# Tables, weights and the first token tiles re-ordered in a spectral mixing kernel with a squared-ReLU MLP behind it

## The chip, the cores and the metric

The kernel runs on one core of a Trainium2 chip. The metric is the device time of one execution in microseconds; before the change its median over 7 runs is 849.89 us (848.02 to 851.43). The engines that compute are TensorE (PE, with its weight loads shown as PEld), VectorE (DVE), ScalarE (ACT) and GpSimd (POOL). SyncE (SP) issues transfers; POOL issues those that convert from 32-bit to 16-bit on the way.

## The reference

Eight batches of 3008 rows with 256 features. Each batch is taken to frequencies along its rows, mixed there by a complex 256 x 256 weight with a bias, shrunk towards zero by 0.01, and taken back. All rows then go through an MLP with 2048 hidden features.

```python
X = np.fft.rfft(x, axis=1)                 # x: (8, 3008, 256)
Xr, Xi = X.real, X.imag
Yr = Xr @ w_r - Xi @ w_i + b_r
Yi = Xr @ w_i + Xi @ w_r + b_i
Y = shrink(Yr, 0.01) + 1j * shrink(Yi, 0.01)   # sign(v) * max(|v| - 0.01, 0)
y = np.fft.irfft(Y, n=3008, axis=1).reshape(24064, 256)
h = y @ w_in                               # 256 x 2048
g = s * np.maximum(h, 0) ** 2 + b
out = g @ w_out                            # 2048 x 256
```

## The kernel before

**The transform.** 3008 is 94 x 32, and the DFT is done in two steps each way. The first step multiplies by a 94 x 96 table (A_t) along n1 and gives 96 rows, kept as 24 pairs; the second goes along n2 (32) with a table for each pair (F_t, and F_2, the same table with its real and imaginary halves exchanged). Mixing follows, then the inverse along n2 (T_t) and the last step along n1 (C_t). The result for one batch is yt: 2 x 128 features on partitions, 32 n2 and 94 n1 as columns. The MLP uses it as it lies.

**Batch 0** has its own routine, first_batch. x comes in four chunks (two halves each) on POOL's queue, the first step writes ut, and then 12 steps run (features in two halves ec of 128, six groups u of four pairs each): mix (W_t; the sums leave as g, half by DVE and half by ACT), fwd_dft (F_t, F_2; ACT makes m and DVE makes z, the shrunk values), inv_dft (T_t, leaves as vt). Four pairs belong to one group, so group 0 uses pairs 0 to 3. turn transposes vt by an identity matrix (eye_t) into vs, and last_dft (C_t) gives yt. Nothing of batch 0 goes through DRAM. In the second half of the steps and behind them, the first DFT step of batch 1 (s1_units, 16 units, each one matmul and one copy to a tile u) is put between; what is left of it goes into the first token tiles.

**Batches 1 to 7** go another way: s1 units store u to DRAM (ud) and load it in another order (us); s23 units do fwd, sum, mix and inverse and store v (vd), which comes back as vs in two loads; s4 units do the last step. One x chunk gives 4 of the 16 s1 units.

**The MLP** goes over token tiles of up to 512 rows. A tile has 16 slots (mc), one for each 128 hidden features. first_mm does the up-projection of a slot (two matmuls into a bank of psh); after every second slot ACT takes the ReLU of the pair (rt), and DVE (or ACT, where a running estimate of load finds it freer) squares it (gt). second_mms does the down-projection of the tile before, four matmuls a slot, into psa, and DVE adds the bias and stores (ost). The first six tiles are "wide": three take the first 16 n2 of batch 0, three the other 16.

**What sets the order.** The dictionary plan holds, for each slot, the units that are emitted ahead of its up-projection; schedule(start, span, units) spreads units evenly over span slots. Batch 1's tiles begin at slot 96 (mark[1]). The framework may then move instructions on each engine's queue within their dependences; each engine works its queue in order. PSUM has eight banks: psf (2) and psa (2), and four that are psm in first_batch and psh (2 x 2) from then on. evac gives a copy out of PSUM to ACT or DVE by the estimate of load.

**Transfers at the start.** SP: A_t, w_r, w_i (whole, 256 KB each, 32-bit staging tiles w_st), the biases, sel_t; after the first chunk of x, F_c (compact forward tables of pairs 0 to 11, L267); after the third chunk, T_t of the first half, F_t and F_2 of pairs 12 to 23, T_t of the second half, and small things (L273 to L283). One-element memsets by DVE (L392, L397) hold these transfers back until then. ACT places W (place_w, L320) and the forward tables of pairs 0 to 11 (place_f, L325; DVE does F_2, L331 and L334). POOL waits at a one-element copy (L406) for F_t of pairs 12 to 23, then issues the four x chunks of batch 1 (L213), w_in in two parts (L291) and w_out (L292). Later it makes W_g from w_st (L311 to L313) and sums w_out (L340 to L345) for the bias matmul (make_bias, L349).

The lines of the steps that matter here: s1 L570, turn L491, last_dft L511, ReLU L776, square L783, up-projection L769, down-projection L840, forward of batches 1 to 7 L606, inverse L665, store of v L674, load of vs L681, last step L718; L170 and L174 are the copies of ACT and DVE.

Of the kernel before, what the change touches and what calls it, by code (L numbers as in the profile page):

```python
# [96 lines left out]
def kernel(  # L97
# [27 lines left out]
    F_d = nc.inline_tensor(fwd[:, 0:H].astype(np.float16), name="dft_fwd").ap()  # L125
    f_all = np.zeros((P, NPAIR, 2, 2, N2))
    t_all = np.zeros((P, NPAIR, 2, 64))
    for i in range(4):
# [3 lines left out]
    f_2 = np.stack([-f_all[:, H:, 1], f_all[:, H:, 0]], axis=2)  # L132
    f_d, f_2_d, t_d = (
        nc.inline_tensor(t.reshape(P, -1, P).astype(np.float16), name=name).ap()
        for t, name in ((f_all[:, H:], "fwd_rest"), (f_2, "fwd_rest_i"), (t_all, "dft_inv"))
# [68 lines left out]
    def emit_load_x(b, first=None):  # L204
        xv = x[b].rearrange("(n1 n2) d -> n1 (n2 d)", n2=N2)
        for c in range(N2 // XCH):
            t = xpool.tile([P, XCH * D], F16, name="x16", tag="x16")
            if first is not None:
                gate = nc.gpsimd.tensor_copy(out=t[0:1, 0:1], in_=first)
            parts = 2 if b == 0 else 1  # L210
            w = XCH * D // parts
            for i in range(parts):
                nc.gpsimd.dma_start(  # L213
                    out=t[0:N1, i * w : (i + 1) * w],
                    in_=xv[:, c * XCH * D + i * w : c * XCH * D + (i + 1) * w],
                )
            x16[(b, c)] = t
# [17 lines left out]
    for w in (w_r, w_i):  # L235
        st = rpool.tile([P, DC, D], F32, name="w_st", tag="rt")
        nc.sync.dma_start(out=st, in_=w.rearrange("(c p) e -> p c e", p=P))
        w_st.append(st)

# [5 lines left out]
    F_c = uspool.tile([P, H, 2, N2], F16, name="F_c", tag="us")  # L245
# [6 lines left out]
    sel_t = cpool.tile([P, P], F16, name="sel_t")  # L252
    eye_t = cpool.tile([P, P], F16, name="eye_t")
# [12 lines left out]
    def emit_load_forward():  # L266
        nc.sync.dma_start(  # L267
            out=F_c.rearrange("p q r k -> p q (r k)"), in_=F_d
        )
        nc.sync.dma_start(out=sel_t, in_=S_d)  # L270

    def emit_load_inverse():
        nc.sync.dma_start(out=T_t[:, 0:H], in_=t_d[:, 0:H])  # L273
        nc.sync.dma_start(out=F_t[:, H:], in_=f_d)
        nc.sync.dma_start(out=F_2[1], in_=f_2_d)
        t_load = nc.sync.dma_start(out=T_t[:, H:], in_=t_d[:, H:])
        with tc.issue_after(t_load.ins):
            nc.sync.dma_start(out=eye_t, in_=E_d)
            nc.sync.dma_start(out=C_t, in_=C_d)
            for i, bv in enumerate((b_r, b_i)):  # L280
                nc.sync.dma_start(out=b_st[:, i], in_=bv.unsqueeze(0).to_broadcast([P, D]))
            nc.sync.dma_start(out=s_bc, in_=moe_s.unsqueeze(0).to_broadcast([P, 1]))
            nc.sync.dma_start(out=bb_bc, in_=moe_b.unsqueeze(0).to_broadcast([P, 1]))  # L283
# [15 lines left out]
    nc.vector.memset(F_t[:, 0:H], 0.0)  # L299
    nc.gpsimd.memset(F_2[0], 0.0)  # L300
# [14 lines left out]
    def blocks(t):  # L315
        return t.rearrange("p q (r a k) -> p q r a k", r=2, a=2)

    def place_w():
        for i in range(2):
            nc.scalar.copy(out=W_t[:, :, i], in_=w_st[i])  # L320

    def place_f():
        for a in range(2):
            r = slice(64 * a, 64 * a + 64)
            nc.scalar.copy(out=blocks(F_t)[r, 0:H, :, a], in_=F_c[r])  # L325

    def place_f_2():

        for a in range(2):
            r = slice(64 * a, 64 * a + 64)  # L330
            nc.vector.tensor_scalar_mul(  # L331
                out=blocks(F_2[0])[r, :, 0, a], in0=F_c[r, :, 1], scalar1=-1.0
            )
            nc.vector.tensor_copy(out=blocks(F_2[0])[r, :, 1, a], in_=F_c[r, :, 0])  # L334
# [28 lines left out]
    def first_batch():  # L363
# [3 lines left out]
        for g in range(N2 // 4):  # L367
# [22 lines left out]
            if c == 0:  # L390
                with tc.issue_after(last_dve.ins):
                    nc.vector.memset(F_c[0:1, 0, 0, 0:1], 0.0)  # L392
                emit_load_forward()
            if c == 2:
                with tc.issue_after(last_dve.ins):
                    for t in (T_t[:, 0:H], F_t[:, H:], F_2[1], T_t[:, H:]):
                        nc.vector.memset(t[0:1, 0, 0:1], 0.0)  # L397
                emit_load_inverse()
            if c == 1:
                with tc.issue_after(last_act.ins):  # L400
                    place_w()
        with tc.issue_after(last_dve.ins), tc.issue_after(last_act.ins):
            place_f()
            place_f_2()

        gate = nc.gpsimd.tensor_copy(out=w_in_t[0][0:1, 0:1], in_=F_t[0:1, H, 0:1])  # L406
        with tc.issue_after(gate.ins):
            emit_load_x(1)
            emit_load_weights()

# [75 lines left out]
        def turn(ec, k):  # L486
            for i in range(2):
                ps = any_bank() if ec else mix_bank()
                n = 8 * k + 4 * i
                for j in range(4):  # L490
                    nc.tensor.matmul(  # L491
                        ps[0:96, j * P : j * P + P], vt[:, ec, n + j, :], eye_t,
                        start=True, stop=True,
                    )
                h, n = divmod(n, HW)
                evac(
                    vs[(0, h)][:, n : n + 4, ec * P : (ec + 1) * P],
                    ps[0:96].rearrange("p (j e) -> p j e", e=P), 512,
                )

        yt = yts[0] = ypool.tile([P, DC, N2, 96], F16, name="yt", tag="yt")

        def last_dft(ec, n2):

            if ec or n2 >= 16:
                ps = [any_bank(), any_bank()]
            else:
                ps = [one_bank(), other_bank()]
            for j in range(8):
                h, k = divmod(n2 + j, HW)  # L510
                nc.tensor.matmul(  # L511
                    ps[j // 4][:, (j % 4) * 96 : (j % 4) * 96 + 96],
                    vs[(0, h)][:, k, ec * P : (ec + 1) * P], C_t,
                    start=True, stop=True,
                )
            for i in range(2):
                evac(
                    yt[:, ec, n2 + 4 * i : n2 + 4 * i + 4, :],
                    ps[i][:, 0:384].rearrange("p (j n) -> p j n", n=96), 384,
                )  # L520
# [9 lines left out]
        for i in range(2 * U + 2):  # L530
# [7 lines left out]
            if 0 <= k < 4:  # L538
                turn(0, k)
            for n in {1: (0,), 2: (8,), 4: (16, 24)}.get(k, ()):  # L540
                last_dft(0, n)
            if i >= 2 * U:
                some(3)
# [7 lines left out]
        for k in range(4):  # L551
            turn(1, k)
            some(1)
            if k:
                last_dft(1, 8 * (k - 1))
        last_dft(1, 24)
        return more

# [308 lines left out]
    with tc.tile_pool(name="psm", bufs=4, space=bass.MemoryType.PSUM) as pool:  # L867
        pools["m"] = pool
        more = first_batch()
# [11 lines left out]
    schedule(0, 10, more)  # L881
    plan.setdefault(15, []).append(make_bias)
    plan.setdefault(17, []).append(load_x_2)
    schedule(24, 42, s23_units(1))
    schedule(mark[1] - 14, 12, s4_units(1))
    for b in range(2, B):
        s0, s1, s2 = mark[b - 2], mark[b - 1], mark[b]
        p = s1 - s0
        schedule(s0 + 40, p - 48, s1_units(b))
# [48 lines left out]
```

## Time and profile before

| | us |
|---|---|
| median of 7 runs | 849.89 |
| the profiled execution | 848.6 |
| its span, first to last instruction | 846.7 |
| first x chunk half of batch 0 used by PE | 5.36 |
| first mixing matmul | 13.77 |
| first forward matmul of batch 0 | 16.55 |
| first s1 matmul of batch 1 | 38.83 |
| w_out used by POOL | 41.94 |
| first up-projection matmul | 48.05 |
| first forward matmul of batch 1 | 63.59 |
| first last-step matmul of batch 1 | 131.01 |

All times in the table and below are from the start of the span. A timeline line gives start, duration, engine, line of the kernel, operation, result and operands, shapes and number; in brackets the engine's idle time ahead of it and what ended that. Busy times of PE count pipelined matmuls, whose ends are modelled, so a full PE can still be one whose matmuls wait for each other. The chain of waits goes back from the last instruction through whatever released each step, by the latest semaphore event seen; a step may be named there that had long been enough.

### The profile page before, as it was taken

How to read it: one execution, taken by the hardware profiler on the slowest of the kernel's cores; microseconds unless marked ns; L12 is line 12 of the kernel's file. 1: busy time of each engine (PE TensorE's matmuls, PEld its weight loads, DVE VectorE, ACT ScalarE, POOL GpSimd, SP SyncE). 2: the span in 40 equal slices, each digit the busy share in tenths (PEclk: the TensorE clock that was granted, in tenths of full speed). 3: DMA queues.
4: the chain of work that ended last, by engine and by line, in shares of the span. 5: the costliest groups of instructions: out<-in, count | busy, mean ns of one | idle time of the engine just before them, and what ended most of it. 6: DMA issues, size and time to landing. Idle time of an engine off the chain costs nothing.

```text
span 846.7 us, 17115 instructions
## 1 busy us (share of the span) xinstructions
PE 834.2 (99%) x6653; PEld 599.7 (71%) x6653; DVE 692.4 (82%) x1026; ACT 642.4 (76%) x864; POOL 45.9 (5%) x71
## 2 busy tenths in 40 slices
PE   8999999999999999999999999999999999999997
PEld 6857767777677766777677776777667777766765
DVE  5989987888878987888888888798977888776674
ACT  5988887787778787788777787778877778666663
POOL 4340000000000001000000000000000000000000
PEclk9999999999999999999999999999999999999999
DMA  8955467224762367324761247613354223411111
GB/s 199 181 144 123 117 144 202 87 71 103 174 185 56 98 164 185 99 74 108 180 178 51 80 102 196 173 41 91 103 154 123 60 78 97 112 33 38 38 44 50
DMA packets 105746, 96.06 MB, mean 113 GB/s; under 512 B 9542, under 2 KB 97482, under 8 KB 104322
## 3 DMA queue, kind: packets, MB, share of 16 engines
q1 hardware_dynamic: 99218, 80.55, 33.1%
q0 software_dynamic: 6448, 14.42, 10.7%
q8 instruction: 52, 0.85, 0.4%
q14 instruction: 28, 0.23, 0.1%
HBM read 53.52 MB, written 46.66 MB: 118 GB/s over the span
## 4 chain that ended last, share of the span: by engine, by line
PE 85%; DMA 5%; DVE 4%; ACT 2%; POOL 1%; issue 1%; DVEq 0%; ACTq 0%; SPq 0%; POOLq 0%
PE psa L840 36%; PE psh L769 35%; PE psf L635 4%; DMA w_out_t<-in_moe_w_out_dram 2%; DVE gt L783 2%; PE psf L570 2%; PE psf L621 2%; PE psf L606 2%; PE psf L718 2%; PE psf L665 2%; ACT rt L776 1%; DMA vd<-v 1%; DMA vs<-vd 1%; DMA x<-in_x_dram 1%; POOL acc L344 1%
## 5 line engine op out<-in xcount | busy, mean ns | idle before, releaser
L776 ACT ACTIVATE rt<-psh 128x1024 f32<-128x1024 f32 (+2 forms) x384 | 386.6, 1008 | 120.3 <-PE psh L769 118.5
L783 DVE TENSOR_TENSOR gt<-rt 128x1024 f16<-128x1024 f32 (+2 forms) x321 | 384.7, 1202 | 98.1 <-ACT rt L776 97.4
L840 PE MATMUL psa<-w_out_t,gt 128*128 128x256 f16 (+1 forms) x3024 | 454.6, 272 | 0.5 <-DVE gt L783 0.4
L840 PEld LDWEIGHTS <-gt 128*128 128x128 f16 (+1 forms) x3024 | 300.9, 101 | 187.8 <-issue 1.7
L769 PE MATMUL psh<-yt,w_in 128*128 128x512 f16 (+1 forms) x1344 | 396.3, 378 | 0.2 <-ACT rt L776 0.2
L769 PEld LDWEIGHTS <-w_in 128*128 128x128 f16 x1536 | 142.9, 98 | 27.9 <-issue 2.4
L850 DVE SCALAR_TENSOR_TENSOR ost<-psa,s_bc,bias_bc 128x512 f32<-128x512 f32 (+2 forms) x97 | 71.1, 733 | 8.3 <-PE psa L840 7.1
L780 ACT ACTIVATE gt<-rt 128x1024 f16<-128x1024 f32 (+2 forms) x63 | 66.2, 1051 | 1.0
L640 DVE TENSOR_TENSOR ring<-psf,s 128x512 f16<-128x512 f32 x84 | 57.6, 686 | 3.7 <-PE psf L635 3.1
L170 ACT CAST v<-psf 128x512 f16<-128x512 f32 x78 | 45.3, 582 | 18.8 <-PE psf L665 18.8
L170 ACT CAST xf<-psf 128x512 f16<-128x512 f32 x82 | 47.9, 585 | 10.9 <-PE psf L606 10.9
L769 PE MATMUL psh<-tail,w_in 128*128 128x512 f16 (+1 forms) x192 | 52.1, 353 | 0.0
L170 ACT CAST u<-psf 96x512 f16<-96x512 f32 x75 | 43.4, 580 | 11.0 <-PE psf L570 10.7
L635 PE MATMUL psf<-W_g,xf 128*128 128x256 f16 x336 | 50.4, 273 | 0.0
L170 ACT CAST yt<-psf 128x480 f16<-128x480 f32 (+2 forms) x73 | 37.3, 523 | 13.7 <-PE psf L718 13.6
L213 POOL DMA_DIRECT2D x<-in_x_dram x36 | 18.7, 526 | 433.3 <-PE psf L570 431.8
L570 PE MATMUL psf<-x,A_t 94*96 94x512 f16 x103 | 39.3, 381 | 1.7 <-ACT yt L170 0.5
L646 DVE TENSOR_TENSOR ring<-ring,high 128x512 f16<-128x512 f16 x84 | 35.6, 424 | 2.3
L647 DVE TENSOR_TENSOR ring<-ring 128x512 f16<-128x512 f16 x84 | 35.6, 423 | 1.9
L645 DVE TENSOR_TENSOR ring<-ring,low 128x512 f16<-128x512 f16 x84 | 35.5, 422 | 1.6
L635 PEld LDWEIGHTS <-xf 128*128 128x128 f16 x336 | 32.9, 98 | 3.8
L718 PE MATMUL psf<-C_t,vs 96*128 96x96 f16 x448 | 33.0, 205 | 0.4 <-DMA vs<-vd 0.2
(97 smaller groups left out, 501.3 us busy)
## 6 DMA issues: line engine op xcount, KB each, us to landing
out_dram<-ost SPq DMA_DIRECT2D x152, 128.0 KB
ud<-u SPq DMA_DIRECT2D x28, 384.0 KB
us<-ud SPq DMA_DIRECT2D x28, 384.0 KB
vd<-v SPq DMA_DIRECT2D x42, 256.0 KB
vs<-vd SPq DMA_DIRECT2D x14, 768.0 KB
x<-in_x_dram POOLq DMA_DIRECT2D x28, 376.0 KB, 6.8
ring<-ring SPq DMA_DIRECT2D x280, 32.0 KB
out_dram<-ost SPq DMA_DIRECT2D x16, 120.0 KB
```

What stands on the lines that cost most here:

```text
L170: return None, nc.scalar.copy(out=dst, in_=src)
L570: nc.tensor.matmul(ps[0:96, :], A_t[0:N1, :], x16[(b, c)][0:N1, j * D : (j + 2) * D], start=True, stop=True,)
L635: nc.tensor.matmul(ps[:, r, :], xt[:, 2 - r, dc], W_g[:, dc, r], start=(dc == 0), stop=(dc == DC - 1),)
L640: nc.vector.tensor_tensor(out=t, in0=ps, in1=hold[i // 2][:, i % 2].unsqueeze(1).to_broadcast([P, 2, D]), op=ALU.add,)
L646: nc.vector.tensor_tensor(out=m, in0=m, in1=high, op=ALU.min)
L718: nc.tensor.matmul(ps[:, j * 96 : (j + 1) * 96], vs[(b, h)][:, k, ec * P : (ec + 1) * P], C_t, start=True, stop=True,)
L769: nc.tensor.matmul(o, w_in_t[dc][:, mc * P : (mc + 1) * P], r, start=(dc == 0), stop=(dc == DC - 1),)
L776: nc.scalar.activation(out=rt[:, :, 0:w], in_=ps[:, :, 0:w], func=AF.Relu)
L780: nc.scalar.activation(out=gt[:, :, 0:w], in_=rt[:, :, 0:w], func=AF.Square)
L783: nc.vector.tensor_tensor(out=gt[:, :, 0:w], in0=rt[:, :, 0:w], in1=rt[:, :, 0:w], op=ALU.mult)
L840: nc.tensor.matmul(ps[0:size, h, :], gts[(ti, mc // 2)][:, mc % 2, sub * size : (sub + 1) * size], w_out_t[:, mc, :], start=(mc == 0), sto ...
L850: nc.vector.scalar_tensor_tensor(out=ost[0:size, 0:k], in0=ps[0:size, 0:k], scalar=s_bc[0:size], in1=bias_bc[0:size, 0:k], op0=ALU.mult, o ...
```

## The change

Four things.

1. The compact forward table F_c holds 4 pairs instead of 12 and is loaded at the very start; the full tables F_t and F_2 are loaded for pairs 4 to 11 too, at the head of the tables that follow the third x chunk. W is loaded and placed by halves of e (128 output features): the first half at the start, the second behind F_t, F_2 and T_t of the first half, its two placing copies (place_w(1)) emitted at step 3. place_f and the first half of W are placed after the second x chunk.
2. POOL issues chunk 0 of batch 1's x, then w_in and w_out, then chunks 1 to 3. Its gate (still F_t of pairs 12 to 23) stands behind more transfers in SP's queue.
3. turn and last_dft work on 4 n2 at a time instead of 8. Only the first 16 n2 of the second feature half are done in first_batch; the other 16 (4 turns and 4 last steps, the list rest) go to slots 20 to 36. Of the s1 units of batch 1, 4 are emitted in first_batch instead of 10 (6 in the last two steps and 4 between the turns); the other 12, instead of 6, go to slots 8 to 20 instead of 0 to 10.
4. make_bias goes to slot 21, the x load of batch 2 to slot 21, s23 of batch 1 to slots 30 to 72 (was 24 to 66), s4 of batch 1 to 83 to 99 (was 82 to 94), s1 of batch 2 to 50 to 88 (was 40 to 88).

```diff
-    F_d = nc.inline_tensor(fwd[:, 0:H].astype(np.float16), name="dft_fwd").ap()
+    F_d = nc.inline_tensor(fwd[:, 0:4].astype(np.float16), name="dft_fwd").ap()
...
-        nc.sync.dma_start(out=st, in_=w.rearrange("(c p) e -> p c e", p=P))
+        nc.sync.dma_start(
+            out=st[:, :, 0:P], in_=w.rearrange("(c p) e -> p c e", p=P)[:, :, 0:P]
+        )
         w_st.append(st)
+    F_c = uspool.tile([P, 4, 2, N2], F16, name="F_c", tag="us")
+    nc.sync.dma_start(out=F_c.rearrange("p q r k -> p q (r k)"), in_=F_d)
...
-    def emit_load_inverse():
+    def emit_load_tables():
+        nc.sync.dma_start(out=F_t[:, 4:H], in_=f_d[:, 0 : H - 4])
+        nc.sync.dma_start(out=F_2[0][:, 4:H], in_=f_2_d[:, 0 : H - 4])
         nc.sync.dma_start(out=T_t[:, 0:H], in_=t_d[:, 0:H])
-        nc.sync.dma_start(out=F_t[:, H:], in_=f_d)
-        nc.sync.dma_start(out=F_2[1], in_=f_2_d)
+        for st, w in zip(w_st, (w_r, w_i)):
+            nc.sync.dma_start(
+                out=st[:, :, P:], in_=w.rearrange("(c p) e -> p c e", p=P)[:, :, P:]
+            )
+        nc.sync.dma_start(out=F_t[:, H:], in_=f_d[:, H - 4 :])
+        nc.sync.dma_start(out=F_2[1], in_=f_2_d[:, H - 4 :])
         t_load = nc.sync.dma_start(out=T_t[:, H:], in_=t_d[:, H:])
...
-    def place_w():
+    def place_w(ec):
+        e = slice(ec * P, ec * P + P)
         for i in range(2):
-            nc.scalar.copy(out=W_t[:, :, i], in_=w_st[i])
+            nc.scalar.copy(out=W_t[:, :, i, e], in_=w_st[i][:, :, e])
...
             if c == 1:
-                with tc.issue_after(last_act.ins):
-                    place_w()
-        with tc.issue_after(last_dve.ins), tc.issue_after(last_act.ins):
-            place_f()
-            place_f_2()
+                with tc.issue_after(last_act.ins), tc.issue_after(last_dve.ins):
+                    place_f()
+                    place_w(0)
...
         with tc.issue_after(gate.ins):
-            emit_load_x(1)
+            emit_load_x(1, chunks=(0,))
             emit_load_weights()
+            emit_load_x(1, chunks=(1, 2, 3))
...
             k = i - U - 2
             if 0 <= k < 4:
-                turn(0, k)
-            for n in {1: (0,), 2: (8,), 4: (16, 24)}.get(k, ()):
+                turn(0, 8 * k)
+                turn(0, 8 * k + 4)
+            for n in {1: (0, 4), 2: (8, 12), 4: (16, 20, 24, 28)}.get(k, ()):
                 last_dft(0, n)
             if i >= 2 * U:
-                some(3)
+                some(2)
+            if i == 3:
+                place_w(1)
...
-        for k in range(4):
-            turn(1, k)
-            some(1)
-            if k:
-                last_dft(1, 8 * (k - 1))
-        last_dft(1, 24)
-        return more
+        for n in range(0, 16, 4):
+            turn(1, n)
+        for n in range(0, 16, 4):
+            last_dft(1, n)
+
+        rest = []
+        for n in (16, 24):
+            rest += [lambda n=n: turn(1, n), lambda n=n: turn(1, n + 4)]
+            rest += [lambda n=n: last_dft(1, n), lambda n=n: last_dft(1, n + 4)]
+        return rest, more
...
-    schedule(0, 10, more)
-    plan.setdefault(15, []).append(make_bias)
-    plan.setdefault(17, []).append(load_x_2)
-    schedule(24, 42, s23_units(1))
-    schedule(mark[1] - 14, 12, s4_units(1))
+    schedule(20, 16, rest)
+    schedule(8, 12, more)
+    plan.setdefault(21, []).append(make_bias)
+    plan.setdefault(21, []).append(load_x_2)
+    schedule(30, 42, s23_units(1))
+    schedule(mark[1] - 13, 16, s4_units(1))
     for b in range(2, B):
         s0, s1, s2 = mark[b - 2], mark[b - 1], mark[b]
         p = s1 - s0
-        schedule(s0 + 40, p - 48, s1_units(b))
+        lead = 50 if b == 2 else 40
+        schedule(s0 + lead, p - lead - 8, s1_units(b))
```

## The prediction

> **What bounds the kernel now.** I read the page's parts 1 and 2 first, then busy time by stage, the chain of waits, and the timelines of the stages that the diff touches.
>
> ```profile
> PE 834.2 (99%) x6653; PEld 599.7 (71%) x6653; DVE 692.4 (82%) x1026; ACT 642.4 (76%) x864; POOL 45.9 (5%) x71
> ```
> ```profile
> 13.80:38.80 25.00, 23.83 (x312) 21.23 (x313) 21.09 (x38) 22.55 (x41) 9.89 (x14) 1.00 0.98 207
> 38.80:48.00 9.20, 7.68 (x87) 5.20 (x85) 8.58 (x17) 8.20 (x18) 5.75 (x5) 1.00 0.53 120
> 48.00:60.00 12.00, 11.54 (x58) 5.38 (x56) 10.82 (x11) 11.16 (x15) 3.92 (x4) 1.00 0.57 162
> 63.60:80.00 16.40, 16.26 (x139) 12.07 (x137) 14.70 (x30) 13.74 (x20) 1.73 (x4) 1.00 0.66 134
> 114.60:131.00 16.40, 16.16 (x109) 10.58 (x108) 13.05 (x14) 11.13 (x14) 0.51 (x1) 1.00 0.77 184
> ```
> The second fence is busy time by stage: stretch, length, then PE, PEld, DVE, ACT, POOL, granted clock, DMA share, GB/s. From 63.6 us on PE is full. Before it, from 38.8 to 60, DVE and ACT are (9 of 10 us), and PE's matmuls are spaced out. The clock is 1.00 everywhere. So only two things move the time: how early PE gets full, and any wait that PE meets later.
>
> The timeline at the first token tile (DVE, then PE):
> ```profile
> 50.30 12.02 DVE L783 TENSOR_TENSOR gt<-rt 128x1024 f16<-128x1024 f32 x10 [1.18 <-ACT rt L776]
> ```
> ```profile
> 60.10 0.39 PE L840 MATMUL psa<-w_out_t,gt 128*128 128x256 f16 x2 [0.39 <-DVE gt L783]
> ```
> Ten squares stand back to back, 1.20 us each, and PE waits for the eighth. The chain of waits at batch 1's last inverse matmul:
> ```profile
> 114.58 0.38 PE psf L665 x2
> ...
> 116.87 6.98 DMA vd<-v
> ...
> 123.99 6.97 DMA vs<-vd
> ...
> 131.01 0.60 PE psf L718 x10
> ```
> The way of batch 1 through DRAM takes 16.43 us and PE's cover for it is just used up (0.24 us of PE idle in that stage). Third, ACT at the start of the mixing:
> ```profile
> 14.82 1.67 ACT L325 COPY F_t<-F_c 64x768 f16<-64x768 f16 x2 [1.11 <-DMA F_c<-dft_fwd]
> 16.52 1.07 ACT L432 CAST g<-psm 128x512 f16<-128x512 f32 x2
> ```
>
> From batch 2's first forward matmul on (148.10 us), PE's instructions stand in the same order in both programs; what the change does is done by then.
>
> **Part 1, tables and W.** Removed: the wait for F_c (1.11 us) and 1.67 us of copies that held up g. At most the first forward matmul goes from 16.55 to 14.85: 1.7 us. Added: a third of the forward table is placed, and the first half of W, while ACT waits for x of batch 0 anyway (it copies 0.48 of every 0.97 us there): nothing, unless x came faster than ACT. x of batch 0 shares its first microseconds with 256 KB less of W and 64 KB more of F_c: some 0.4 us. But what F_c brought now comes in SP's queue at about 11.6: F_t 256 KB, F_2 256, T_t 384, W 128 and 128, F_t 384, F_2 384. Before, the first two (T_t and F_t, 768 KB) were issued from 12.04 on, and F_t's landing let POOL go on at 17.69: 768 KB in 5.65 us. At that pace 768 KB are in at 17.25; the rest at 300 GB/s (between the 243 and 357 that the 2 us stages from 14 to 18 show): the halves of W, up to 1024 and 1152 KB, land at about 18.1 and 18.6. ACT meets the first copy of the second half of W (two of about 0.4 us) between the g of group 2 and the m of group 1; m, z and every later step of ACT queue behind it. m of group 1 was at 19.01; it comes at about 18.5, the second copy follows, and vt, at 19.80 before, at about 19.5. I take -0.3; bounds -1.7 (no new wait) and +0.8 (both copies and the later table in full).
>
> **Part 2, weights ahead of x.** POOL's gate is the landing of F_t's last half: 1536 KB into the queue instead of 768, so 19.9 instead of 17.69. The seven transfers behind it end 2.2 us later, 44.1 instead of 41.88 (21.38 + 20.5, the landing of w_out), but w_out now lands before three x chunks of 1.8 us each (376 KB at the 209 to 215 GB/s of the stages from 24 to 34), at about 38.7. Chunks 1 to 3 land at 40.5, 42.3 and 44.1. PE needs them at about 42.5, 45 and 49 (part 3). Cost nothing; the cover is 2.0 us at chunk 1, which stands ahead of the first up-projection in PE's order: past that it costs one for one. The sums of w_out on POOL (10.2 us) end at about 48.9, the bias matmul is at 57: its 0.16 us at most goes. The chain's 27 us on w_out and POOL would have promised more, but PE is not idle there.
>
> **Part 3, work moved into the tiles.** PE's order is the same up to the first matmul of batch 1's DFT (38.83). From there to the first up-projection (48.05) there were 15 u copies, 8 turns, 1 vt and 8 yt copies. Start to start a 512-column copy takes 0.47 on ACT and 0.60 on DVE, 0.264 side by side; 384 columns 0.37 and 0.465, so 0.206. Sum 24 x 0.264 + 8 x 0.206 = 8.0 in 9.22 us. After: 6 + 4 + 1 and 4: 3.7, with the same slack 4.3 us. The first up-projection comes 4.9 us earlier, 43.1. The squares start 2.25 later as before (50.30 - 48.05), at 45.4; in DVE's order two u copies now stand among the first eight: 8 x 1.2 + 2 x 0.6 = 10.8, the eighth is done at 56.2 instead of 59.9: 3.7 earlier. But at this point (the 15th down-projection matmul) PE had done 42 up-projection matmuls and now has done 40 (0.43), the bias (0.11) and the moved 4 turns and 4 last steps (4 x 0.22 + 4 x 0.17 = 1.56) are still to come: 2.1. Gain 1.6. The moved copies (3.8 us over two engines) then lie in the second tile, where DVE and ACT have 2 of 16 us free each; nothing. Bounds: +0.2 (only the 1.9 us of the moved copies gained, against 2.1) and -2.8 (the whole 4.9 kept).
>
> Batch 1's us: last DFT matmul 49.77, landed by 62.3. Now 56.4 and 68.9, the first quarter some 3.9 us earlier, 65.0; the first forward matmul (slot 30) comes at 56.4 + 10.2 = 66.6. Hidden, by 1.6 us.
>
> **Part 4, the later schedule.** Between the last inverse matmul of batch 1 and its first last-DFT matmul lie 12 slots instead of 17: 12 x 0.43 (up) + 12 x 0.44 (down) + 5 x 0.22 = 11.5 us; the same count gave 15.9 before where PE was busy for 16.16, so 11.7. What it has to cover: matmul, copy and issue (2.29 before, of which SP was 2.04 in two output stores that now come after: I take 1.5), vd, vs. vd's last store took 6.98 here; from its issue to that of vs the seven batches show 7.1, 5.7, 2.9, 3.9, 3.9, 2.4 and 2.6. A load of x and a ud store were in the same queues in batch 1, and will be again, but the two output stores will not: I take the median, 3.9. vs 6.97. Sum 12.3: PE waits 0.6, less the 0.24 that it waited before: +0.35. Bounds: -0.24 (covered) and +3.9 (15.6 with the vd of before).
> [...]
>
> The last steps of batch 1 go over 16 slots instead of 12; there the chain runs through ACT and DVE from 135.3 to 138.6. I take -0.3 (bounds -0.5, 0).
>
> **Sum.** -0.3 - 1.6 + 0.35 - 0.3 = -1.85 us. The profiled execution took 848.6 us (span 846.7), 1.3 below the median of 849.89; its span becomes 844.9, the median 848.0.
>
> **Rivals.**
> - The trip through DRAM is not covered: vd takes as long as in batch 1 before. Part 4 is +3.9, the sum +1.7: 851.6, slower. From a trip of 14.2 us (11.7 + 0.24 + the 2.2 that the rest gives) it decides. For: vd's row of this same batch; against: six other batches.
> - Little moves: ACT's copies of W wait and part 3 gives only half: +0.3 - 0.8 + 0.35 - 0.3 = -0.45, 849.4. For: DVE stays the limit of the first tile.
> - The start gives all: -1.0 - 2.6 - 0.24 - 0.5 = -4.3, 845.6. For: DVE and ACT had 1 us free of 9 and 12 us in both stages.
> - x chunk 1 is late: it needs more than 2.0 us of further delay in the stream and costs what lies over it: 4 us of delay give +2.0, the sum 850.0. For: the tables ahead of it doubled. Against: the stream's pace is steady.
>
> **How the numbers follow.** The sum as above 0.40, a quarter of it within 0.2%; the start gives all 0.18; little moves 0.18; trip not covered, or x late, 0.24. The range 845.3 to 852.0 goes from the case that gives all to the uncovered trip. 0.2% is 1.7 us, about what a measurement can tell: faster 0.48 (0.30 + 0.18), within 0.26 (0.10 + 0.16), slower 0.26. If the likeliest holds, 846.5 to 849.0.
>
> **What would show it.** Right: first up-projection at 43 to 44; squares from 45.4 with two u copies among them; PE full from 56; ACT waiting 0.5 to 1 us for w_st near 18; w_out landing near 38; PE idle under 1 us before L720. Wrong: PE idle of 2 to 4 us at L720 with vd or vs as releaser; PE waiting for x ahead of the first up-projection; the first forward matmul of batch 1 waiting for us; first up-projection after 45.

## The result and the profile after

The changed kernel takes 856.64 us (median of 12 runs, 851.88 to 858.0) where the kernel before takes 849.42 on the same chip: a ratio of 1.0077 (95% interval 1.0066 to 1.0089). It is slower by 0.8%, and outside the range. The profiled execution took 858.0 us, the longest of the twelve; its span is 856.2.

Some marks tell where each kernel's profiled execution stands; they are worked out from the starts of the instructions' records, one execution each. The runs named in the table are described below. The first column is the first matmul of batch 1's first DFT step (us). Then comes ACT's ReLU of slots 1, 79, 87 and 103, against the kernel before (+ is later). From slot 103 on, the same work is done and the order is the same in all, while up to there a kernel may be earlier because it has left work for later. The last column is the stretch from the first mark to the last: every kernel has the same work to do in it, but for the extra matmuls of a_awake and best_1.

```
                first s1  slot 1      79      87     103   stretch
before             38.83    +0.0    +0.0    +0.0    +0.0     115.4
changed            38.46    -4.5    +2.6    +8.9    +9.0     124.8
a_s4_late          38.34    -4.6    +1.4    -0.4    +1.4     117.2
a_awake            38.02    -4.9    -0.4    +3.0    +3.1     119.3
a_short_sum        38.38    -4.5    +0.1    +4.9    +5.0     120.8
b_cover_12         38.82    +0.0    +3.0    +2.8    +2.7     118.1
a_x3_late          38.74    -4.2    +0.9    +0.3    +1.1     116.5
a_sched_before     38.12    -4.8    -0.1    -0.3    -0.6     115.5
best_1             37.56    -5.2    -0.3    -2.0    -0.4     116.2
c_s4_wout          38.35    -4.6    -1.0    -2.8    -1.2     114.7
c_sched_wout       38.86    -4.1    +0.2    +0.7    +0.4     115.7
b_wout             38.73    -0.1    -0.6    -0.8    -0.8     114.6
b_part1            37.57    -1.3    +1.1    +0.9    +0.9     117.5
b_part1_bias       38.24    -0.6    +7.9    +7.7    +7.7     123.6
b_part1_wout       37.65    -1.2    -1.7    -1.9    -1.9     114.6
b_part2            38.75    -0.1    -0.6    -0.6    -0.6     114.8
b_part12           38.30    +3.5    +3.0    +2.8    +2.8     118.7
```

The changed kernel starts its tiles 4.5 us earlier, has lost that and 2.6 more by slot 79, and loses another 6.4 us by slot 87. The views of the profile say how. One caution: a_s4_late and a_awake have the changed kernel's order of work up to slot 79 and stand 1.2 and 3.0 us ahead of it there, so a part of the 2.6 belongs to this one execution.

The start came as forecast. ACT's timeline has the wait for the first half-copy of W's second half (predicted 0.5 to 1 us), and the first up-projection is at 43.16 us (48.05 before). DVE's timeline at the first tile, and below it that of POOL (start, duration, what):

```profile
18.68 0.40 ACT L325 CAST W_t<-w_st 128x256 f16<-128x256 f32 x1 [1.21 <-DMA w_st<-in_w_r_dram]
```
```profile
44.01 0.69 DVE L174 CAST u<-psf 96x512 f16<-96x512 f32 x1 [0.43 <-PE psf L572]
45.85 4.18 DVE L785 TENSOR_TENSOR gt<-rt 128x1024 f16<-128x1024 f32 x2 [1.16 <-ACT rt L778]
49.95 0.67 DVE L174 CAST u<-psa 96x512 f16<-96x512 f32 x1
50.55 5.75 DVE L785 TENSOR_TENSOR gt<-rt 128x1024 f16<-128x1024 f32 x5
56.22 0.67 DVE L174 CAST u<-psa 96x512 f16<-96x512 f32 x1
56.83 2.34 DVE L785 TENSOR_TENSOR gt<-rt 128x1024 f16<-128x1024 f32 x2
```
```profile
39.54 1.15 POOL L341 TENSOR_TENSOR acc<-w_out_t 128x512 f32<-128x512 f16 x1 [4.04 <-DMA w_out_t<-in_moe_w_out_dram]
40.77 8.18 POOL L345 TENSOR_TENSOR acc<-acc,w_out_t 128x512 f32<-128x512 f32 x6
49.02 1.59 POOL L346 TENSOR_TENSOR w_sum<-acc 128x256 f16<-128x256 f32 x1
```

The first two squares took 2.08 and 2.17 us, not 1.21: they lie beside the last of POOL's adds over w_out, one of which took 2.02 us instead of 1.15. The eighth square ended at 58.0 us, 1.8 later than forecast. A copy out of PSUM beside the same adds took 0.69 us (44.01), one without them 0.67 (56.22). The price differs between executions. From the first up-projection to the end of the eighth square the changed kernel takes 14.9 us. a_awake, a_s4_late and a_x3_late, the same program up to there, take 14.0, 14.4 and 14.5, and two kernels whose adds are out of the way (a_short_sum, c_s4_wout) 13.1. So the adds cost 1.0 to 1.8 us here. In the kernel before, POOL's adds were nearly done when the squares began at 50.30, and one of the squares took 1.75:

```profile
43.16 7.31 POOL L344 TENSOR_TENSOR acc<-acc,w_out_t 128x512 f32<-128x512 f32 x6
```

The second loss is at the trip of batch 1's v through DRAM. The chain of waits, and busy time by stage (length, then PE, PEld, DVE, ACT, POOL, TensorE's granted clock, where 1.00 is full speed, DMA share, GB/s):

```profile
116.51 5.56 DMA vd<-v
122.15 0.59 ACT v L170
...
123.14 5.50 DMA vd<-v
128.71 9.50 DMA vs<-vd
138.25 0.58 PE psf L720 x5
...
139.26 0.80 PE psh L771 x2
```
```profile
114.60:131.00 16.40, 15.25 (x103) 9.90 (x102) 13.16 (x23) 12.29 (x18) 1.03 (x2) 1.00 0.70 162
...
134.00:138.00 4.00, 0.39 (x4) 0.10 (x1) 1.16 (x1) 0.12 (x1) 0.00 (x0) 0.96 1.00 225
138.00:144.00 6.00, 5.75 (x31) 3.46 (x32) 1.72 (x2) 2.60 (x5) 0.00 (x0) 0.50 0.33 119
144.00:146.00 2.00, 2.00 (x19) 1.45 (x18) 0.71 (x2) 1.41 (x2) 0.51 (x1) 0.88 0.42 20
```
```profile
PE psf L720 <- DMA vs<-vd: 3.9, 1, 3.9
PE psf L572 <- ACT v L170: 1.2, 1, 1.2
```

The last fence is PE's waits there (us in total, times, longest). The last inverse matmul is at 121.25 us. ACT's copy of its result had to wait 0.93 us for a free buffer v, because a store issued at 116.51 took 5.56; then the last store took 5.5 and the loads 9.5: 17.0 us in all, counted as in the prediction, where the kernel before had 16.4. So the trip is hardly longer than it was; the slots that cover it are fewer. The 1.2 us that PE waits behind ACT's copy lie ahead of slot 79 and are part of the 2.6 there. PE ran out of work at 134.4 and stood still for 3.9 us. And then something that stands in no row of the profile before: the granted clock fell to half at 137.7 and stayed there until 144.5. Two up-projection matmuls that take 0.41 us (a_awake, at the same place) took 0.80.

### The profile page after: what moved, and what is told of

Same layout as the page of the kernel before. It is cut to its first block, busy times and chain, and to the rows that moved or that the text cites. A ratio compares the mean times of both kernels' runs of the same rounds, so it can differ in the third digit from the quotient of the medians.

```text
span 856.2 us, 17129 instructions
## 1 busy us (share of the span) xinstructions
PE 837.8 (98%) x6653; PEld 600.6 (70%) x6653; DVE 694.2 (81%) x1030; ACT 641.3 (75%) x866; POOL 45.2 (5%) x70
## 4 chain that ended last, share of the span: by engine, by line
PE 87%; DMA 5%; DVE 3%; ACT 3%; issue 1%; POOL 0%; SPq 0%; DVEq 0%; ACTq 0%; POOLq 0%
PE psa L842 35%; PE psh L771 35%; PE psf L637 4%; PE psf L572 2%; PE psf L720 2%; PE psf L608 2%; PE psf L623 2%; PE psf L667 2%; DVE gt L785 2%; DMA ring<-ring 2%; DMA vd<-v 1%; ACT rt L778 1%; DMA vs<-vd 1%; DMA x<-in_x_dram 1%; PE psm L424 1%
## 5 line engine op out<-in xcount | busy, mean ns | idle before, releaser
L720 PE MATMUL psf<-C_t,vs 96*128 96x96 f16 x448 | 34.0, 208 | 3.9 <-DMA vs<-vd 3.9
```

What stands on the lines that cost most here:

```text
L720: nc.tensor.matmul(ps[:, j * 96 : (j + 1) * 96], vs[(b, h)][:, k, ec * P : (ec + 1) * P], C_t, start=True, stop=True,)
```

## The experiments

Each kernel ran on one chip beside the kernel before; ratios are to that. Theory 1: the uncovered trip and the clock behind it are the loss. Theory 2: POOL's adds eat what the start gains. The rivals stand in the expectations.

**a_s4_late: the last step of batch 1 five slots later.**

```diff
-    schedule(mark[1] - 13, 16, s4_units(1))
+    schedule(mark[1] - 8, 16, s4_units(1))
```


> The changed kernel with batch 1's last DFT step (s4) begun at slot 88 instead of 83, so that 17 slots stand between the last inverse matmul of batch 1 and it, instead of 12. Theory 1 (the trip of v through DRAM is uncovered: 3.9 us of idle TensorE, and the granted clock that falls behind it to 0.50 for 6 us): idle ahead of L720 under 0.3 us, granted clock 1.00 from 128 to 160 us, time 848.5 to 851. Rival A (the wait only moves to the token tile at slot 96, which needs y): idle of 2 us or more ahead of a first matmul on yt, 853 or more. Rival B (what was lost was lost in the start and the first tiles): 855.5 to 857.

850.5 us, ratio 1.0015 (1.0006 to 1.0024). Busy time by stage, the same two stretches:

```profile
134.00:138.00 4.00, 4.00 (x34) 2.85 (x32) 2.44 (x4) 2.91 (x5) 0.51 (x1) 1.00 0.96 230
138.00:144.00 6.00, 6.00 (x63) 4.45 (x61) 4.71 (x7) 4.39 (x8) 0.00 (x0) 1.00 0.67 195
```

No idle, no fall of the clock, and four fifths of the loss gone with one number. The trip itself is still long (some 17 us, and PE still waits 1.1 us for ACT's copy of v); it is only covered.

**a_awake: TensorE kept busy in the wait.**

```diff
             ps = one_bank()
+            if b == 1 and g == 0:
+                for _ in range(72):
+                    nc.tensor.matmul(ps[:, 0:P], ones, ones, start=True, stop=True)
```


> The changed kernel with 72 matmuls of 128x128 on constants (about 4 us, nothing reads them) put on TensorE ahead of batch 1's first s4 matmul: the wait for vs stays, TensorE is not idle in it. If the idle stretch is what drops the granted clock (0.50 from 138 to 144 us): clock 1.00 there, 2.5 to 3.5 us gained, about 853.5. Rival (the fall of the clock has another cause, or costs nothing in the end): 856 to 857, clock 0.5 to 0.9 between 136 and 146 us as before.

853.41 us, ratio 1.0044 (1.0028 to 1.0059). PE's timeline shows the matmuls in place of the wait:

```profile
131.31 4.18 PE L720 MATMUL psf<-ones 128*128 128x128 f16 x72
135.32 0.38 PE L723 MATMUL psf<-C_t,vs 96*128 96x96 f16 x5
```

The clock stays at 1.00. Between 1.0077 and 1.0044 lie 2.8 us: that is what the half clock costs, on top of the time that PE stood still. With four runs of a_awake the difference is uncertain by some 1.6 us either way, but the marks agree: from slot 79 to 103 the changed kernel loses 6.4 us and a_awake 3.5. The mean granted clock, recorded for every run, is 0.995 to 0.998 in all twelve of the changed kernel and 0.999 or 1.000 in all four of a_awake. The idle stretch is its cause.

**a_short_sum: POOL's six adds cut to one.**

```diff
-        for q in range(4, MC, 2):
+        for q in range(4, 6, 2):
```


> The changed kernel with the sum over w_out on GpSimd cut from six adds to one; it leaves out five sixths of that sum, so the output is not the reference's. Theory 2 (these adds beside the first squares make a square 2.1 instead of 1.21 us, which ate the 1.9 us that the start had gained): first two squares at 1.2 us, eighth square ends 1.5 to 2 us earlier, time 854 to 855.3. Rival (the first squares are lost time only where the trip through DRAM does not set the end): squares as quick, time within 0.8 us of 856.6.

854.42 us, ratio 1.0062 (1.0045 to 1.0078). The first two squares, in DVE's timeline:

```profile
45.77 2.36 DVE L785 TENSOR_TENSOR gt<-rt 128x1024 f16<-128x1024 f32 x2 [1.16 <-ACT rt L778]
```

2.36 us for two instead of 4.18. So it is the adds. By slot 79 this kernel is 2.5 us ahead of the changed one, but a_awake, with the adds in it, is 3.0 ahead there, so that mark cannot tell the price. By the ratios it is 1.3 us ahead at the end, with overlapping intervals; the wait of 3.9 us for vs is still there, but the clock stayed at half for 3.4 us only, not 6.8, and that is part of the 1.3.

**b_cover_12: the kernel before with as few slots for the trip.**

```diff
-    schedule(24, 42, s23_units(1))
+    schedule(29, 42, s23_units(1))
```


> The kernel before with batch 1's second and third step stretched to slot 70, so that 12 slots stand between its last inverse matmul and its s4 at slot 82, as in the changed kernel; nothing else is changed. Theory 1: 2.5 to 4.5 us of idle TensorE ahead of the s4 matmuls and a granted clock under 0.9 behind it, time 853 to 857. Rival (12 slots suffice in the kernel before, and the trip is long in the changed one only by its other transfers): idle under 1.2 us, clock 1.00, 849 to 851.

850.84 us, ratio 1.0024 (1.0014 to 1.0033). The rival holds: 12 slots between the last inverse matmul and s4 sufficed here. PE did not wait for vs and the clock stayed at 1.00. The last store of v was issued at 123.20 and the loads at 126.04, so it took 2.8 us against 5.5. Theory 1 has to be narrowed: 12 slots are too few for a trip of 17 us and enough for one under 12, and the length of the trip depends on what lies beside it. What this kernel did lose (3 us by slot 71) is not the trip. 0.9 of it is its first squares (2.19 and 1.74 us; w_out landed 0.9 us later than in the kernel before, though the program is the same up to there). PE also waited 0.9 for POOL's sum at the bias matmul; where the rest went was not followed.

**a_x3_late: two loads of x kept out of the trip.** In the changed kernel the chunks of batch 3 that take the buffers of batch 2's first step are issued at 116.45 and 128.24, just ahead of a store of v and of the loads of vs. In the kernel before two of them stand beside the trip as well, ahead of its last store (116.87) and of its loads (123.99):

```profile
110.39 0.51 POOL L213 DMA_DIRECT2D x<-in_x_dram  x1 [14.25 <-PE psf L570]
122.86 0.51 POOL L213 DMA_DIRECT2D x<-in_x_dram  x1 [11.95 <-PE psf L570]
```

```diff
-            plan.setdefault(s1 + 6, []).append(lambda b=b: emit_load_x(b + 1))
+            plan.setdefault(s1 + 6, []).append(
+                lambda b=b: emit_load_x(b + 1, vs[(1, 1)][0:1, 0, 0:1] if b == 2 else None)
+            )
```


> The changed kernel with the loads of x of batch 3 held back until vs of batch 1 has landed (in the changed kernel two of them were issued at 116.45 and 128.24 us, beside the first and behind the last of v's stores). Theory 3 (these loads made the trip 17.0 us): the copy of v no longer waits 0.9 us, the trip is 13.5 us or less, idle ahead of L720 under 1 us, 850 to 852.5. Rival (v's own four stores, the 384 KB store of ud and two stores of results, bunched in 7 us, are what is slow): idle of 2.5 us or more, 854 to 857.

851.98 us, ratio 1.0029 (1.0011 to 1.0048). In the profiled execution (849.81, the quickest of five) nobody waits for v or vs, and the last store of v takes 2.3 us (issued 122.56, loads issued 124.90). PE begins the last step at 132.6 without a wait, so the loads took at most 7.7 us and the trip at most 12. So without the x loads the trip is at least 5 us shorter. The other profiles agree as to the store: in all but this one and b_cover_12 a chunk of batch 3's x is issued 5.9 to 7.4 us ahead of the last store, and that store takes 4.8 to 7.6 us; in b_cover_12 it is 11.4 us ahead, and the store takes 2.8. For the loads of vs it is less clear: in b_cover_12 a chunk was issued 0.2 us ahead of them, and they took at most 7.6 us, not 9.5. The other runs of a_x3_late are 1 to 3 us longer; there is no trace of those.

**a_sched_before: part 4 undone.** The 12 later s1 units go back to slots 0 to 10 as well; the bias stays at slot 21.

```diff
-    schedule(8, 12, more)
+    schedule(0, 10, more)
...
-    plan.setdefault(21, []).append(load_x_2)
-    schedule(30, 42, s23_units(1))
-    schedule(mark[1] - 13, 16, s4_units(1))
+    plan.setdefault(17, []).append(load_x_2)
+    schedule(24, 42, s23_units(1))
+    schedule(mark[1] - 14, 12, s4_units(1))
...
-        lead = 50 if b == 2 else 40
-        schedule(s0 + lead, p - lead - 8, s1_units(b))
+        schedule(s0 + 40, p - 48, s1_units(b))
```


> The changed kernel with part 4 undone: the slots of batch 1's first DFT step, of the loads of batch 2, of s23, of s4 and of batch 2's first step are those of the kernel before; the loads, tables and the end of batch 0 in the tiles stay as changed. So parts 1 to 3 alone. Theory 1 and 2 (the loss is the trip of v through DRAM; the gain of the start is eaten by squares beside GpSimd's adds): idle ahead of L720 under 0.5 us, clock 1.00, 848.5 to 850.5. By the sum of the prediction (parts 1 to 3: -1.9): 847 to 848.2. Rival (the start itself costs): 852 or more.

849.37 us, ratio 1.001 (1.0001 to 1.0018). Nearly all of the loss was part 4. But parts 1 to 3 win nothing either, where the sum had them at -1.9.

**best_1, c_s4_wout, c_sched_wout, b_wout: POOL's adds out of the way.** best_1 is a_s4_late with the sum over w_out made by 12 accumulating matmuls with ones at slot 6. The c kernels are a_s4_late and a_sched_before with w_out loaded ahead of w_in; b_wout is the kernel before with that alone.

```diff
+        nc.gpsimd.dma_start(
+            out=w_out_t, in_=moe_w_out.rearrange("(mc p) d -> p mc d", p=P)
+        )
         for dc in range(DC):
             nc.gpsimd.dma_start(out=w_in_t[dc], in_=moe_w_in[dc * P : (dc + 1) * P, :])
-        nc.gpsimd.dma_start(
-            out=w_out_t, in_=moe_w_out.rearrange("(mc p) d -> p mc d", p=P)
-        )
```


> The changed kernel with s4 from slot 88, and the sum over w_out made on TensorE: 12 matmuls by ones, accumulated, at slot 6, in place of GpSimd's six adds. Theories 1 and 2 together: no idle ahead of L720, squares of 1.2 us from the first, 847 to 849. Rival (the 12 matmuls, 1.3 to 2.5 us of TensorE, cost what the squares give): 849.5 to 851.

> The changed kernel with s4 from slot 88 and with w_out loaded ahead of w_in, so that GpSimd's sums over it begin some 3 to 4 us earlier and end before the first squares. Theory 2 (the squares lose to GpSimd's adds): squares of 1.2 us from the first on, eighth square 1.3 to 1.9 us earlier than in the changed kernel, 847.5 to 849.3. Rival (the sums then lie beside the evacuations at 36 to 44 us and slow these as much, or w_in comes too late for the first up-projection): first up-projection later than 43.9, or evacuations over 10% longer, 850 or more.

> The changed kernel with part 4 undone (the slots of the kernel before) and w_out loaded ahead of w_in. By a_sched_before (ratio 1.001, the squares beside GpSimd's adds still in it) less 1.3 to 1.9 us: 847.3 to 848.5, 0.1 to 0.2 per cent under the kernel before. Rival (what the first tiles gain is waited for again at x of batch 1 or at vs): 849 or more.

> The kernel before with w_out loaded ahead of w_in and nothing else. Theory 2: its first squares (1.26 and 1.75 us beside the last sums) fall to 1.2, a gain of at most 0.5 us: 848.8 to 849.4. Rival (w_in, landing at 41 instead of 36.6 us, or the sums beside the evacuations, cost more): 850 or more.

best_1 849.43 us, ratio 1.0005 (0.9996 to 1.0014); c_s4_wout 848.35, 0.9995 (0.9987 to 1.0004); c_sched_wout 848.26, 0.9992 (0.9983 to 1.0001); b_wout 848.16, 1.0 (0.9987 to 1.0013). In c_s4_wout POOL's timeline ends ahead of the squares, and DVE's squares are whole:

```profile
36.59 7.32 POOL L345 TENSOR_TENSOR acc<-acc,w_out_t 128x512 f32<-128x512 f32 x6
43.98 0.73 POOL L346 TENSOR_TENSOR w_sum<-acc 128x256 f16<-128x256 f32 x1
```
```profile
45.73 2.36 DVE L785 TENSOR_TENSOR gt<-rt 128x1024 f16<-128x1024 f32 x2 [1.16 <-ACT rt L778]
...
54.89 2.35 DVE L785 TENSOR_TENSOR gt<-rt 128x1024 f16<-128x1024 f32 x2
```

The eighth square ends at 56.1, where the prediction had 56.2, and the evacuations beside the adds did not suffer: DVE's copy of 384 columns took 0.56 us at 42.91, and in the kernel before, ahead of its adds, 0.55 and 0.54 (39.10 and 39.57). From a_s4_late (1.0015) to this (0.9995) are 1.7 us, uncertain by some 1.1; that fits the 1.0 to 1.8 us that the adds cost the first squares. best_1, whose 12 matmuls are work for TensorE, comes out between its theory and its rival. The last column of the table of marks has the lesson: b_wout, without any of the change, has the stretch of c_s4_wout (114.6 and 114.7); the 115.7 of c_sched_wout is from the longest of its eleven executions.

**b_part1 and b_part1_bias: the tables and the halves of W alone.** Both have part 1 of the change on the kernel before; the second asks for the bias at slot 21 instead of 15.

```diff
-    plan.setdefault(15, []).append(make_bias)
+    plan.setdefault(21, []).append(make_bias)
```


> The kernel before with the tables and the halves of W alone (part 1): x of batch 1, the first tiles and the schedule as before. By the prediction's sum -0.3 us: 848.7 to 849.5 where before has 849.4. Rival (the later halves of W and the split tables hold up batch 0, or the start of the tiles): first up-projection later than 48.05, 850 or more.

> The kernel before with part 1 (tables, halves of W) as in the run of part 1 alone, but with the bias made at slot 21 as in the changed kernel, instead of 15. In part 1 alone TensorE waited 3.0 us at slot 15 for GpSimd's sum over w_out. Theory 4 (part 1 alone lost only by that wait, and in its longer runs by the clock behind it): no wait for w_sum, 848.5 to 849.8. Rival (part 1 loses elsewhere, such as in the loads of x of batch 1, 1.5 us later): 851 or more.

854.25 us, ratio 1.0074 (1.006 to 1.0088), and 856.16, ratio 1.0086 (1.0073 to 1.0099): as slow as the whole change, in another place. PE's waits, first of b_part1, then of b_part1_bias:

```profile
PE psa L350 <- POOL w_sum L346: 3.0, 1, 3.0
```
```profile
PE psa L350 <- POOL w_sum L346: 6.3, 1, 6.3
```

and POOL's timeline and the busy time by stage of b_part1_bias:

```profile
45.38 1.15 POOL L341 TENSOR_TENSOR acc<-w_out_t 128x512 f32<-128x512 f16 x1 [10.08 <-DMA w_out_t<-in_moe_w_out_dram]
46.61 9.90 POOL L345 TENSOR_TENSOR acc<-acc,w_out_t 128x512 f32<-128x512 f32 x6
```
```profile
54.00:58.00 4.00, 0.00 (x0) 0.00 (x0) 3.59 (x2) 0.00 (x0) 3.84 (x3) 0.89 0.69 194
58.00:62.00 4.00, 3.77 (x10) 1.47 (x10) 0.60 (x1) 1.50 (x2) 0.17 (x1) 0.50 0.74 199
```

The longer tables push w_out back (landed at 41.87 before, 42.78 and 45.3 here), POOL sums later, its sum collides with the squares, and TensorE comes to the bias matmul too early. In the kernel before the sum is done only 0.06 us ahead of that matmul. b_cover_12, where w_out lands at 42.80 without part 1, waits 0.9; b_part1, whose tiles also start 1.3 us earlier, waits 3.0. The slot asked for was no help: the framework put the matmul behind the 16th up-projection matmul all the same, so this run did not take the wait away as meant. In b_part1's profiled execution (849.29, 3.0 us of idle) the clock did not fall; its other runs took 853.5 to 856.4, with a mean granted clock of 0.995 to 0.998 against 1.000, and no trace tells what else they lost.

**b_part1_wout, b_part2 and b_part12: what remains of parts 1 and 2.** Part 1 with w_out ahead of w_in; part 2 alone (the lines of the change itself); both parts, without 3 and 4.

> The kernel before with part 1 (tables, halves of W) and w_out loaded ahead of w_in, so that GpSimd's sum over w_out is done before TensorE comes to the bias matmul. Theory 4 (part 1 alone lost by TensorE's wait for that sum, 3.0 and 6.3 us in the two profiles, and by the clock behind it): no wait for w_sum, clock 1.00 from 50 to 80 us, and part 1 is worth the 0.3 us of the prediction's sum over the kernel before with w_out first: 847.5 to 848.8. Rival (part 1 loses elsewhere): 850 or more, with the wait gone.

> The kernel before with part 2 alone: chunk 0 of batch 1's x, then w_in and w_out, then chunks 1 to 3. By the stream's pace w_out lands near 36.5 and the chunks near 38, 40 and 42 us; the sum over w_out ends before the first squares. By the prediction's sum nothing is lost: 848.3 to 849.4. Rival (x of batch 1 comes too late for the 10 first-step units ahead of the first up-projection): a wait of TensorE for x of 1 us or more, first up-projection after 48.6, 850 or more.

> The kernel before with parts 1 and 2 of the change, without 3 and 4 (the end of batch 0, batch 1's first step and the schedule as before). If the two add up (part 2 alone was 0.6 us quicker at slot 23 than before, part 1 with w_out first 1.7): no wait for w_sum, 1.5 to 1.9 us quicker from slot 23 on, 847.0 to 848.2, the quickest version here. Rival (batch 1's x, held up by the longer stream of tables as well, now comes too late for the ten first-step units ahead of the first up-projection): TensorE waits for x 1 us or more, 849.5 or more.

b_part1_wout 847.33 us, ratio 0.9989 (0.9975 to 1.0004); b_part2 847.9, 0.9988 (0.9979 to 0.9998); b_part12 849.89, 1.0013 (1.0002 to 1.0023). With the wait for the sum gone, part 1 has b_wout's stretch (114.6) and starts it earlier. Part 2 alone gains what b_wout gains in the table of marks, and by the same thing: its squares take 1.22 us from the first. Both together lose, as the rival said. PE's waits in b_part12, and its busy time by stage:

```profile
PE psm L570 <- DMA x<-in_x_dram: 1.9, 1, 1.9
```
```profile
39.00:40.00 1.00, 0.33 (x2) 0.07 (x1) 1.00 (x3) 1.00 (x4) 0.64 (x1) 1.00 1.10 221
40.00:41.00 1.00, 0.00 (x0) 0.00 (x0) 0.18 (x1) 0.54 (x2) 0.92 (x2) 0.94 1.05 209
41.00:42.00 1.00, 0.76 (x2) 0.30 (x2) 0.00 (x0) 0.14 (x1) 0.92 (x2) 0.50 0.95 201
...
47.00:48.00 1.00, 1.00 (x14) 0.72 (x13) 0.63 (x2) 0.64 (x2) 0.92 (x2) 0.65 0.78 201
```

Chunk 1 of batch 1's x lands at 41.2 us, and without part 3 it is wanted at 39.3. The wait is 1.9 us, and the clock is at half for 6.8 us behind it.

By the ratios no version beats the kernel before by more than 0.12%, and neither of the two quickest, b_part2 and b_part1_wout, has parts 3 or 4. b_part2's interval alone lies wholly under it, by less than the 0.2% that the prediction took for what a measurement can tell; b_part1_wout has the shortest median and the shortest span (844.7).

## Why the prediction was wrong

**Part 4 failed, in three terms of "what it has to cover" and in one that was missing.** The cover was right: 11.7 us predicted; PE's work ran out 13.1 us behind the last inverse matmul, and 1.2 of these were its wait for v. The need was predicted as 1.5 + 3.9 + 6.97 = 12.3 (12.4 by its own terms) and was 1.9 + 5.6 + 9.5 = 17.0. The median over seven batches was the wrong row for the store: batch 1's own row, 7.1, had the company that it was to have again, two loads of batch 3's x, and without these the store takes 2.3 (a_x3_late). The prediction named "a load of x", and then took the median all the same. That the loads of vs could take longer than 6.97 was not considered; why they took 9.5 is not fully settled. The missing term is the price of an idle TensorE: 2.8 us of half clock behind 3.9 us of idle (a_awake). The rival "the trip through DRAM is not covered" was the right mechanism, and its sign, 2 to 4 us of idle at L720, came. That its price, +3.9, equals the wait there is luck: it set a need of 15.6 against a cover of 11.7, where 17.0 stood against 13.1. It left out the 1.2 us of the wait for v and the 2.8 of the clock.

**Part 3 failed twice: in one duration, and in what it counted as gain.** First up-projection 43.1, measured 43.16; squares from 45.4, measured 45.85. "8 x 1.2" failed: two of the eight took 2.1 because POOL was adding. The trace before had the row: one of the ten squares, which the prediction gives as 1.20 us each, took 1.75 us, beside POOL. The change moved the squares 4.5 us earlier and the adds only 2.4, and so onto each other. With the adds out of the way (c_s4_wout) the eighth square came at 56.1, against the 56.2 of the prediction; that mechanism was right.

But "Gain 1.6" was not there even then. Over the stretch to slot 103, c_s4_wout takes 114.7 us and b_wout, which has no part 3, 114.6. Summed over the stretch, PE's idle time is 1.4 us in the first and 2.2 in the second (2.7 in the kernel before), but its busy time, for as many matmuls, is 113.3 and 112.4. The 0.8 us of idle that are gone in c_s4_wout come back as longer matmul time. No run has part 3 alone; that it wins nothing is read from kernels that hold it together with other parts. The prediction had priced the moved work at 2.1 us of bare matmuls and had credited 3.7 us for an earlier square; the idle time that there was to win, 2.7 us in the whole stretch, was never set beside that sum. Why the matmuls are busy longer was not settled. The -0.3 for the wider s4 was not measured alone.

Beside POOL's adds the square went from 1.21 us to as much as 2.0 to 2.2, while a copy out of PSUM stayed at 0.67 to 0.69. Why the one suffers and the other does not was not shown.

**Part 1 was sized about right, and its danger was missed.** -0.3 was taken; the first matmul of batch 1's first step came 0.37 us earlier in the changed kernel. Over the thirteen profiles with part 1 it lies between 37.56 and 38.86, in the middle 38.30, so -0.5, against 38.73 to 38.83 in the four without; the spread among the thirteen, 1.3 us, is larger than the gain. ACT's wait for W (1.21 us, predicted 0.5 to 1) was there and cost little. But the line on the bias ("its 0.16 us at most goes") held only with part 2 beside it: part 1 alone makes TensorE wait for that sum, 3.0 and 6.3 us in the two profiles.

**Part 2 kept its times, but "cost nothing" left out a gain.** By bringing w_out forward it frees the first squares of the kernel before: 0.6 us (b_part2). w_out was forecast at 38.7 and in use at 39.5; the chunks at 40.5, 42.3 and 44.1 landed at 41.3, 43.2 and 45.2. PE did not wait for them, because part 3 had moved the units that need them. In b_part12 the cover of chunk 1 is gone, and there the prediction's "it costs one for one" fails: a wait of 1.9 us, with the half clock behind it, puts slot 1 4.7 us behind b_part1_wout.

**Batch 1's first forward matmul** was forecast at 66.6 and came at 68.68; in c_s4_wout, with the adds out of the way, it came at 66.75.

## What to carry to other kernels

A move has two sides: the work that is moved, and the transfers and adds that come to lie beside something new; look up, for each, what it will run beside at its new time, and take the duration from a row with that company, not from a median. Price a wait of TensorE together with the matmuls that may follow it at half clock, which here made 3.9 us cost 6.4 to 6.7; the clock did not fall behind every such wait (3.0 us in b_part1's profile left it alone). Parts of a change can need each other: part 1 alone lost 0.7 to 0.9% (and nothing once w_out was loaded first), parts 1 and 2 without part 3 lost 0.1%, and each was safe only by a cover that something else gave.

## What was not expected of the hardware

- **The clock.** In all seventeen profiles every stretch at one granted clock lasts a whole number of 3.41 us, but for the one that the end of the program cuts off: 133.12 us at full clock ahead of the fall in the changed kernel are 39 of them. The granted clock fell to 0.50, 3.3 us (changed kernel) and 3.5 us (a_short_sum) after the last matmul, and the half-speed stretch lasted 6.8, 3.4, 6.8 (b_part1_bias) and 6.8 us (b_part12): once or twice the same 3.4. In b_part12 it fell only 1.5 us after the matmuls stopped, and PE was idle for 1.9; in b_part1, 3.0 us of idle left it at 1.00. b_cover_12, b_wout and b_part2 have a half-speed stretch of 3.4 us in the first step of batch 0 (from 10.16, 8.77 and 9.20 us), where PE never stood still for more than 1.0 us; their mean granted clocks are 0.998, 0.997 and 0.998. In the 3.4 us ahead of the falls in b_part12 and in these three PE was busy for 0.52 to 0.57 of the time. So these falls came without a wholly idle stretch, and the 3.0 us of idle in b_part1 brought none; what decides was not tested.
- **Squares beside adds.** A DVE square of 128 x 1024 goes from 1.21 us to as much as 2.0 to 2.2 while POOL adds 128 x 512 in 32 bits, and one such add goes from 1.15 to 2.02.
